# Side work of layer 1 tied on VectorE behind the two adds of each group

## The chip, the cores and the metric

The kernel runs on one core of a Trainium2 chip. The metric is the device time of one execution in microseconds (us); lower is better. PE is TensorE's matmul stream, PEld its weight loads, DVE is VectorE, ACT is ScalarE, POOL is GpSimd, SP is the engine whose queue issues all the DMAs.

## The reference

Three stages follow each other on 4608 tokens:

```python
# block-diagonal attention, chunks of 64, 8 heads of 64
attn = softmax(scale * q_c @ k_c.T); x = attn @ v_c         # [4608, 512]
# layer 1: 512 -> 2048 -> 512
r = maximum(x @ w_in, 0); x = (s * r * r + b) @ w_out
# layer 2: 512 -> 2048 -> 512, a rational function of h
h = x @ w2_in
g = (a0 + a1 h + a2 h^2 + a3 h^3) / (1 + |b0| |h| + |b1| h^2 + 1e-6)
out = g @ w2_out
```

Inputs are float32; the weights of layer 1 and 2 come in as 64-bit numbers, which DVE turns into float32 by shifts.

## The kernel before, in words

Every matrix product is made of float16 pairs (high and low part, three products each). The first product of a layer goes by a Strassen scheme: seven products p1 to p7 of half-size blocks, each 12 matmuls of 256 columns (L446), summed in two PSUM banks Z and Y. The second product (`l1_y2`, L485) has 48 matmuls of 512 columns per group.

Layer 1 runs over ten blocks j of tokens. Blocks 0 and 1 (256 tokens each) go in plain float32 while the weights are decoded. Blocks 2 to 9 (512 tokens) take four groups u = 0 to 3 each, `l1_group`; these 32 groups are called **G0 to G31** here (Gn is block 2 + n // 4, u = n % 4). PE's work in one group, in order: p1, p7, 15 matmuls L485 of the group before, p2, p6, 15 more, p4, p5, 12 more, p3, 6 more. Between them stand small matmuls of the attention of later blocks: the scores (L264) and the products with v (`at_pv`, L312).

Two adds on DVE close p4 and p5: L519 adds p7 to bank Y, **L520** adds it to bank Z. p3 writes bank Z, so PE may start p3 only after L520; the 12 matmuls L485 before p3 are what PE has to do meanwhile. On ACT each group has two evacuations after p1 and p7 (L505, L506), two after p2 and p6 (L513, L514; p4 needs L514), one after p3 (L527), and for each half of the group a Relu, a square and a cast (L522, L492, L493), whose result DVE reads (L494).

Everything else in layer 1 is side work: attention of later blocks (`at_*`: L275 and L276 subtract a maximum, L277 exp, L284 to L291 probabilities, L247 and L248 the split of v, L316 and L317 the result x), the split of x into pieces (`x_piece`, L402 to L416; pieces for p1, p7, p2, p5, p6, p4, p3 in this order), the output y of the block before (`y_norm`, `y_piece`, L567, L402 to L416), decoding and parking layer 2's weights (`w2_park`: L142, L144, L145, L586, then a DMA; one raw buffer of two units, loaded again by SP after every second unit), and constants of layer 2 (`l2_consts`, L658 to L677, 24 instructions on one or a few columns). These jobs are put in slots by hand, 16 slots per block, four per group; `jobs_at(n, c)` in `l1_group` issues slot n of the group, and its ACT instructions are queued behind the ACT instruction c.

The order on each engine is made at build time by a list scheduler with a cost model: the program's order gives the priority, but an instruction that looks ready early may be pulled ahead of others. `tc.issue_after(ins)` forbids that: what is issued in it on the engine of `ins` stands behind `ins` in that engine's queue. No time is spent by it on the chip; it is an order alone. The queues of DVE, ACT and PE then run in that order.

Of the kernel before, what the change touches and what calls it, by code (L numbers as in the profile page):

```python
# [13 lines left out]
ALU = mybir.AluOpType  # L14
# [6 lines left out]
def attn_moe_moe2(ctx: ExitStack, tc: tile.TileContext, qk, v, w_in, w_out, s_in, b_in,  # L21
# [57 lines left out]
    V, A, G, T = nc.vector, nc.scalar, nc.gpsimd, nc.tensor  # L79
# [358 lines left out]
    def product(w, x, u, p, b, start, stop=False):  # L438
        wk, pk = PROD[p]
        for s in range(2):  # L440
            f = 2 * u + s
            for kk in range(2):
                t = w.sh[wk, kk, f // 4]
                for n, (a, l) in enumerate(TERMS):
                    o = (f % 4) * 128
                    T.matmul(out=b[:, s, :], lhsT=t[:, a, o:o + 128], rhs=x[pk][:, l, kk, :],  # L446
                             start=start and s + kk + n == 0, stop=stop and s + kk + n == 4,
                             skip_group_check=True)
# [26 lines left out]
    crit = {}  # L475
# [14 lines left out]
    def l1_half(h, g):  # L490
        hf = h.rearrange("p s b t -> p (s b t)")
        A.activation(out=hf, in_=hf, func=AF.Square)  # L492
        A.activation(out=g[:, 0], in_=hf, func=AF.Copy)  # L493
        V.tensor_tensor(out=g[:, 1], in0=hf, in1=g[:, 0], op=ALU.subtract)  # L494

    def l1_group(j, u, jobs_at, m2):
        x = xhl[j]
        bank = lambda nm: ps_h.tile([128, 2, 256], F32, name=nm, tag="h")
        half = lambda: l1_p.tile([128, 2, 2, 256], F32, name="h1", tag="h1")
        jobs_at(0, crit.get("h"))  # L500
        Z, Y = bank("bZ"), bank("bY")
        product(wi1, x, u, "1", Z, True)
        product(wi1, x, u, "7", Y, True)
        p7 = l1_p.tile([128, 2, 256], F32, name="sn", tag="sn", bufs=3)
        A.activation(out=p7, in_=Y, func=AF.Copy)  # L505
        c = A.activation(out=Y, in_=Z, func=AF.Copy)  # L506
        m2(0)
        jobs_at(1, c)
        product(wi1, x, u, "2", Y, False)
        product(wi1, x, u, "6", Z, False)  # L510
        h0, h1 = half(), half()
        g = gq[j, u] = g_p.tile([128, 2, 2, 1024], F16, name="g", tag="g")
        A.activation(out=h0[:, :, 0], in_=Y, func=AF.Relu, scale=16.0 * C1)  # L513
        c = A.activation(out=Y, in_=Z, func=AF.Copy)  # L514
        m2(1)
        jobs_at(2, c)
        product(wi1, x, u, "4", Y, False, True)
        product(wi1, x, u, "5", Z, False)
        V.tensor_tensor(out=h1[:, :, 0], in0=Y, in1=p7, op=ALU.add)  # L519
        V.tensor_tensor(out=h1[:, :, 1], in0=Z, in1=p7, op=ALU.add)  # L520
        h1f = h1.rearrange("p s b t -> p (s b t)")
        A.activation(out=h1f, in_=h1f, func=AF.Relu, scale=16.0 * C1)  # L522
        l1_half(h1, g[:, :, 1])
        m2(2)
        jobs_at(3, c)
        product(wi1, x, u, "3", Z, False, True)
        crit["h"] = A.activation(out=h0[:, :, 1], in_=Z, func=AF.Relu, scale=16.0 * C1)  # L527
        l1_half(h0, g[:, :, 0])
        m2(3)
        if u == 3:  # L530
            xhl.pop(j)
# [62 lines left out]
    def w2_fetch(q):  # L594
        kk, g = q
        t = raw_p.tile([128, 4, 512], F32, name="wq", tag="raw")
        for i, u in enumerate(((kk, g), (kk + 2, g), (kk, g + 2), (kk + 2, g + 2))):
            nc.sync.dma_start(out=t[:, i, :], in_=wi2.dr[u])
        quad[q] = t
# [28 lines left out]
    def w2_combo(q, p):  # L628
        combo(wi2, [quad[q][:, i, :] for i in range(4)], q, p, (w2sc, w2nsc), w2_p if q[1] == 0 else wi1a_p, ws_raw)
# [101 lines left out]
    def run_jobs(slot):  # L731
        for fn, args in jobs.pop(slot, []):
            fn(*args)
# [21 lines left out]
    for j in range(NFULL, NB):  # L755
        at(start[j] + 3, l1_alpha, j)
        slot = start[j] + 1 - (PV0 if j > NFULL else P0)
# [48 lines left out]
    if True:  # L806
# [95 lines left out]
        def l1_slot(slot, after):  # L902
            j, k = slot // KF, slot % KF
            with tc.issue_after(after.ins) if after else ExitStack():
                run_jobs(slot)
            if j == NB - 1:
                if k >= 6:
                    wo2.fetch(wo2.todo.pop(0))
                if k >= 8:
                    wo2.split(wo2.cut.pop(0))  # L910
                for n in range(28 * k // KF, 28 * (k + 1) // KF):
                    q = quads[n // 7]
                    w2_combo(q, WORD[n % 7])
                    if n % 7 == 6 and n // 7 + 1 < 4:
                        w2_fetch(quads[n // 7 + 1])

        for j in range(NFULL, NB):
            if j == NB - 1:
                right.close()
                w2_p = ctx.enter_context(tc.tile_pool(name="w2", bufs=14, side="right", reuse_waits="tile"))  # L920
                w2_fetch(quads[0])
            for u in range(4):
                l1_group(j, u, lambda n, c: l1_slot(start[j] + 4 * u + n, c), m2_of(prev))
                prev = (j, u)
# [17 lines left out]
        def new_bank(i, k):  # L942
            pool, tag = {"Z": (ps_h, "h"), "Y": (ps_a, "s"), "C": (ps_a, "x")}[k]
            bank[i, k] = pool.tile([128, 2, 256], F32, name="b" + k, tag=tag)
            return bank[i, k]
# [76 lines left out]
        for i in range(N):  # L1022
            for q in range(4):
                step, slot = i + 2, q
                if i == 0:
                    step, slot = ((2, 2), (2, 3), (2, 3), (3, 0))[q]
                elif i == 1:
                    slot = q
# [21 lines left out]
        for i in range(N + 2):  # L1050
            cur, c = i < N, i - 1
            sl = (parts if c in (0, N - 1) else full) if 0 <= c < N else []
            if cur:
# [5 lines left out]
                Z, Y = new_bank(i, "Z"), new_bank(i, "Y")  # L1059
# [73 lines left out]
```

## Time and profile before

| what | value |
|---|---|
| time, median of 3 runs | 1589.96 us (1589.4 to 1591.37) |
| profiled execution, its own time | 1589.04 us |
| its span in the profile | 1587.2 us |
| PE busy over the span | 1538.0 us (97%) |
| DVE busy over the span | 1314.2 us (83%) |
| layer 1 in blocks 2 to 9 (G0 to G31) | about 160 to 870 us |
| layer 2 | about 870 to 1587 us |

How to read it: PE is busy nearly all the time, so time is saved where PE waits or runs at the lower clock. A row of the timeline gives the start, the duration, the engine, the line, what is written and read, how many instructions were merged into the row, and in brackets the idle time of the engine before it and what released it. A row of matmuls starts when the first is issued; the next row starts when PE issues the next one, so the difference of two starts is the time a piece of work takes in the stream.

### The profile page before, as it was taken

What the parts mean: (1) busy time and instruction counts of PE and PEld (TensorE: products, weight loads), DVE (VectorE), ACT (ScalarE), POOL (GpSimd) and SP (SyncE); (2) the same over time, 40 slices, a digit from 0 to 9 for tenths busy, and PEclk for the clock granted to TensorE, in tenths of its full rate; (3) what the DMA queues carried; (4) which work ended last, traced back from release to release, by engine and by line L of the source; (5) the groups of instructions that cost most, each with busy time, mean ns of one, the idle gap of its engine ahead of it and who ended that gap; (6) DMA issues with size and microseconds to landing.
All of it is one profiled execution on the core that took longest, in us unless ns stands there. A gap on an engine that the chain in (4) does not pass through costs nothing.

```text
span 1587.2 us, 29579 instructions
## 1 busy us (share of the span) xinstructions
PE 1538.0 (97%) x12497; PEld 1040.0 (66%) x12501; DVE 1314.2 (83%) x1980; ACT 963.2 (61%) x1268; POOL 25.4 (2%) x57
## 2 busy tenths in 40 slices
PE   7999999899899999999999899999999999999998
PEld 6878666566566666666666665666666666666664
DVE  7987989889877666665685999999888999999887
ACT  3565957556566666665675765555656565656564
POOL 0000000000000000000000000000000000000000
PEclk8999999999999999999999999999999999999999
DMA  7731345555532231312143020101010101011000
GB/s 283 274 87 55 93 138 160 197 167 172 174 101 87 61 95 29 106 28 54 47 133 114 13 75 34 47 27 47 27 47 28 47 27 47 31 44 35 26 27 27
DMA packets 86118, 131.43 MB, mean 83 GB/s; under 512 B 39648, under 2 KB 39648, under 8 KB 85984
## 3 DMA queue, kind: packets, MB, share of 16 engines
q1 hardware_dynamic: 85984, 129.53, 26.0%
q8 instruction: 98, 1.61, 0.4%
q14 instruction: 36, 0.29, 0.1%
HBM read 86.77 MB, written 34.34 MB: 76 GB/s over the span
## 4 chain that ended last, share of the span: by engine, by line
PE 59%; DVE 26%; DMA 5%; ACT 5%; issue 4%; SPq 0%; POOL 0%; DVEq 0%; ACTq 0%; POOLq 0%
PE y L1004 18%; PE bZ L446 15%; PE y L485 12%; PE bY L446 9%; PE bC L446 2%; DVE wf L145 2%; DVE bits L144 2%; DMA raw<-in_moe_w_in_dram 2%; DMA raw<-in_moe_w_out_dram 1%; DVE bits L142 1%; DVE whl L622 1%; DVE e L972 1%; DVE e L992 1%; DVE e L971 1%; DVE v L986 1%
## 5 line engine op out<-in xcount | busy, mean ns | idle before, releaser
L446 PEld LDWEIGHTS <-whl 128*128 128x128 f16 x5712 | 556.8, 98 | 145.4 <-issue 33.5
L446 PE MATMUL bZ<-xhl,whl 128*128 128x256 f16 x3264 | 405.8, 275 | 19.7 <-DVE h L520 14.8
L1004 PE MATMUL y<-whl,g 128*128 128x512 f16 x1728 | 396.2, 379 | 4.8 <-DVE g L993 3.5
L485 PE MATMUL y<-g,whl 128*128 128x512 f16 x1536 | 356.0, 382 | 0.1
L1004 PEld LDWEIGHTS <-g 128*128 128x128 f16 x1728 | 168.6, 98 | 180.7 <-DVE g L993 5.0
L485 PEld LDWEIGHTS <-whl 128*128 128x128 f16 x1536 | 151.3, 98 | 156.2 <-issue 3.4
L446 PE MATMUL bY<-xhl,whl 128*128 128x256 f16 x2016 | 248.5, 273 | 3.8 <-ACT h L527 1.7
L1093 ACT ACTIVATE h<-bZ 128x512 f32<-128x512 f32 x36 | 21.5, 597 | 226.5 <-PE bZ L446 172.6
L494 DVE TENSOR_TENSOR g<-h,g 128x1024 f16<-128x1024 f32 x64 | 78.2, 1222 | 54.8 <-ACT g L493 54.5
L970 DVE SCALAR_TENSOR_TENSOR v<-v,c 128x2048 f32<-128x2048 f32 (+1 forms) x42 | 85.8, 2044 | 33.0 <-ACT v L961 33.0
L522 ACT ACTIVATE h<-h 128x1024 f32<-128x1024 f32 x32 | 33.8, 1057 | 114.7 <-DVE h L520 114.7
L971 DVE TENSOR_TENSOR e<-e,h 128x2048 f32<-128x2048 f32 (+1 forms) x42 | 83.1, 1981 | 11.8 <-ACT e L962 11.7
L985 DVE SCALAR_TENSOR_TENSOR g<-e,na,r 128x2048 f16<-128x2048 f32 (+1 forms) x42 | 85.7, 2045 | 5.6 <-ACT r L977 2.5
L972 DVE SCALAR_TENSOR_TENSOR e<-e,na,h 128x2048 f32<-128x2048 f32 (+1 forms) x42 | 85.8, 2045 | 0.9
L992 DVE SCALAR_TENSOR_TENSOR e<-e,na,v 128x2048 f32<-128x2048 f32 (+1 forms) x42 | 85.6, 2042 | 0.7
L962 ACT ACTIVATE e<-h,na 128x2048 f32<-128x2048 f32 (+1 forms) x42 | 77.3, 1842 | 11.5 <-DVE g L993 11.4
L986 DVE SCALAR_TENSOR_TENSOR v<-v,g 128x2048 f32<-128x2048 f32 (+1 forms) x42 | 83.2, 1984 | 0.9
L961 ACT ACTIVATE v<-h,bc 128x2048 f32<-128x2048 f32 (+1 forms) x42 | 73.7, 1758 | 15.1 <-DVE h L1087 14.1
L993 DVE TENSOR_TENSOR g<-e,r 128x2048 f16<-128x2048 f32 (+1 forms) x42 | 82.8, 1976 | 0.0
L976 ACT ACTIVATE r<-v,c 128x2048 f32<-128x2048 f32 (+1 forms) x42 | 73.5, 1755 | 3.9 <-DVE v L970 3.9
L977 ACT ACTIVATE r<-r,c 128x2048 f32<-128x2048 f32 (+1 forms) x42 | 73.5, 1757 | 1.0
L493 ACT ACTIVATE g<-h 128x1024 f16<-128x1024 f32 x64 | 67.4, 1053 | 1.0
(189 smaller groups left out, 1808.1 us busy)
## 6 DMA issues: line engine op xcount, KB each, us to landing
qk<-in_qk_dram SPq DMA_DIRECT2D x36, 512.0 KB, 3.9
raw<-in_moe_w_in_dram SPq DMA_DIRECT2D x16, 1024.0 KB, 5.9
raw<-in_moe_w_out_dram SPq DMA_DIRECT2D x16, 1024.0 KB, 5.2
v<-in_v_dram SPq DMA_DIRECT2D x36, 256.0 KB, 2.7
out_dram<-o SPq DMA_DIRECT2D x36, 256.0 KB, 2.1
yd<-yhl SPq DMA_DIRECT2D x27, 256.0 KB, 2.1
xhl<-yd SPq DMA_DIRECT2D x27, 256.0 KB, 2.6
w2din<-wf SPq DMA_DIRECT2D x16, 256.0 KB, 2.1
```

What stands on the lines that cost most here:

```text
L446: T.matmul(out=b[:, s, :], lhsT=t[:, a, o:o + 128], rhs=x[pk][:, l, kk, :], start=start and s + kk + n == 0, stop=stop and s + kk + n == 4 ...
L485: T.matmul(out=ybank[j][dd], lhsT=wo1.hl[f][:, o:o + 128], rhs=g[:, l], start=(first and m == 0), stop=(last and m == 2))
L494: V.tensor_tensor(out=g[:, 1], in0=hf, in1=g[:, 0], op=ALU.subtract)
L962: A.activation(out=e, in_=hh, func=AF.Identity, scale=na[:, 3:4], bias=na[:, 2:3])
L970: V.scalar_tensor_tensor(out=v, in0=v, scalar=dlt, in1=v, op0=ALU.add, op1=ALU.mult)
L971: V.tensor_tensor(out=e, in0=e, in1=hh, op=ALU.mult)
L972: V.scalar_tensor_tensor(out=e, in0=e, scalar=na[:, 1:2], in1=hh, op0=ALU.add, op1=ALU.mult)
L985: V.scalar_tensor_tensor(out=g[:, 0], in0=e, scalar=na[:, 0:1], in1=r, op0=ALU.add, op1=ALU.mult)
L986: V.scalar_tensor_tensor(out=v, in0=v, scalar=q0c, in1=g[:, 0], op0=ALU.add, op1=ALU.mult)
L992: V.scalar_tensor_tensor(out=e, in0=e, scalar=na[:, 0:1], in1=v, op0=ALU.add, op1=ALU.subtract)
L993: V.tensor_tensor(out=g[:, 1], in0=e, in1=r, op=ALU.mult)
L1004: T.matmul(out=ybank[j][t], lhsT=g[:, a, q, t * 128:(t + 1) * 128], rhs=w[:, l * 512:(l + 1) * 512], start=(u + q == 0 and m == 0), stop=( ...
```

## The change

`jobs_at(2, c)`, the third slot's side work, is issued after the two adds and no longer ahead of p4. And the second add (now L519 in the changed file, L520 before) is kept as `crit["v"]`; all side work of a slot is put behind the latest such add on DVE. So slots 2 and 3 of a group stand behind this group's adds, slots 0 and 1 behind those of the group before. The weights' last steps in block 9 (`wo2.split`, `w2_combo`) stay outside.

```diff
         c = A.activation(out=Y, in_=Z, func=AF.Copy)
         m2(1)
-        jobs_at(2, c)
         product(wi1, x, u, "4", Y, False, True)
         product(wi1, x, u, "5", Z, False)
         V.tensor_tensor(out=h1[:, :, 0], in0=Y, in1=p7, op=ALU.add)
-        V.tensor_tensor(out=h1[:, :, 1], in0=Z, in1=p7, op=ALU.add)
+        crit["v"] = V.tensor_tensor(out=h1[:, :, 1], in0=Z, in1=p7, op=ALU.add)
+        jobs_at(2, c)
...
         def l1_slot(slot, after):
             j, k = slot // KF, slot % KF
             with tc.issue_after(after.ins) if after else ExitStack():
-                run_jobs(slot)
+                with tc.issue_after(crit["v"].ins) if "v" in crit else ExitStack():
+                    run_jobs(slot)
```

The changed file has one line less ahead of the adds, so lines 517 to 520 before are 516 to 519 after; L513 and L514 keep their numbers. The order of the instructions moves at these places.

DVE before, the end of G5: a decode of layer 2's weights (`bits`) stands between the two adds of h_3753.

```order
L288 TENSOR_TENSOR e<-e,rs 128x512
L416 SCALAR_TENSOR_TENSOR yhl<-tx,c_256,yhl 128x512
L108 TENSOR_SCALAR inv<-ape 128x1
L408 TENSOR_TENSOR tx<-y_3557 128x512
L109 RECIPROCAL sc<-inv 128x1
L519 TENSOR_TENSOR h_3753<-bY,sn 128x2x256
L142 TENSOR_SCALAR bits<-raw 128x512
L144 SCALAR_TENSOR_TENSOR bits<-raw,bits 128x512
L520 TENSOR_TENSOR h_3753<-bZ,sn 128x2x256
L145 SCALAR_TENSOR_TENSOR wf<-raw,bits 128x512
```

DVE after, the same two adds (L518 and L519 here) and what follows them.

```order
L109 RECIPROCAL c_256<-c_248 128x1
L570 TENSOR_SCALAR c_256<-c_256 128x1
L518 TENSOR_TENSOR h_3753<-bY,sn 128x2x256
L519 TENSOR_TENSOR h_3753<-bZ,sn 128x2x256
L275 TENSOR_REDUCE mx<-sp 128x4 x2
L276 TENSOR_TENSOR e<-sp,mx 128x4x64 x2
L416 SCALAR_TENSOR_TENSOR yhl<-y_3557,c_256,yhl 128x512
L402 TENSOR_TENSOR tx<-y_3557 128x512
L104 TENSOR_SCALAR apm<-amx 128x1
L142 TENSOR_SCALAR bits<-raw 128x512
```

The next group's decode, which was pulled ahead of the second add, now comes ten rows behind it; the adds stand together in nearly all groups.

DVE after, the end of G4 (h_3376): constants of layer 2 (c_269 and c_270 are two of their columns) stand between the side work and the adds. Before, these 24 instructions stood among the first decodes of the kernel, near 30 to 46 us.

```order
L288 TENSOR_TENSOR e<-e,rs 128x512
L675 TENSOR_SCALAR c_269<-c_269 128x1
L408 TENSOR_TENSOR tx<-y_1999 128x512
L673 RECIPROCAL c_270<-c_269 128x1
L291 TENSOR_TENSOR ph<-e,ph 128x512
L674 SCALAR_TENSOR_TENSOR c_269<-c_270,gb,c_269 128x1
L411 TENSOR_TENSOR y_1999<-tx,y_1999 128x2x256
L675 TENSOR_SCALAR c_269<-c_269 128x1
L416 SCALAR_TENSOR_TENSOR yhl<-tx,c_256,yhl 128x512
L673 RECIPROCAL c_270<-c_269 128x1
L518 TENSOR_TENSOR h_3376<-bY,sn 128x2x256
L674 SCALAR_TENSOR_TENSOR c_269<-c_270,gb,c_269 128x1
```

G4's stretch of DVE's queue, from the adds of G3 to those of G4, grows from 49 to 72 instructions.

ACT in G11 (u = 3, h_5556), around the evacuations L513 and L514, first before:

```order
L505 ACTIVATE sn<-bY 128x512
L506 ACTIVATE bY<-bZ 128x512
L290 ACTIVATE ph<-e 128x512
L415 ACTIVATE xhl<-x_4606,c_242 128x512
L415 ACTIVATE xhl<-tx,c_242 128x512
L513 ACTIVATE h_5556<-bY 128x2x256
L514 ACTIVATE bY<-bZ 128x512
L277 ACTIVATE e<-e 128x512
```

And ACT after, the same place:

```order
L505 ACTIVATE sn<-bY 128x512
L506 ACTIVATE bY<-bZ 128x512
L247 ACTIVATE vs<-v,sc 128x512
L415 ACTIVATE xhl<-x_4632,c_242 128x512
L415 ACTIVATE xhl<-tx,c_242 128x512
L290 ACTIVATE ph<-e 128x512
L513 ACTIVATE h_5556<-bY 128x2x256
L514 ACTIVATE bY<-bZ 128x512
```

L513 and L514 now stand behind L290, and on DVE L290's input (L288) and the scale c_242 (L392) have moved to the end of the group's queue, while before c_242 stood in its first half. All u = 3 groups from G7 to G23 have this order.

## Rows read from the trace of the kernel before

**Rows 1.** What PE waited for, 205 to 880 us (total, times, longest).

```profile
PE bZ L446 <- DVE h L520: 14.8, 6, 4.6
PE bY L446 <- ACT h L527: 1.7, 4, 0.9
PE bY L446 <- ACT bY L506: 1.1, 2, 0.6
```

**Rows 2.** Timeline of DVE at the end of G5.

```profile
286.73 0.43 DVE L142 TENSOR_SCALAR bits<-raw 128x512 int32<-128x512 int32 x1 [3.50 <-DMA raw<-in_moe_w_in_dram]
287.19 0.69 DVE L144 SCALAR_TENSOR_TENSOR bits<-raw,bits 128x512 int32<-128x512 int32 x1
287.80 0.68 DVE L520 TENSOR_TENSOR h<-bZ,sn 128x512 f32<-128x512 f32 x1
```

**Rows 3.** Timeline of PE: the 12 L485 of G1, p3 of G4, G5, G9.

```profile
187.48 2.75 PE L485 MATMUL y<-g,whl 128*128 128x512 f16 x12
261.66 1.47 PE L446 MATMUL bZ<-xhl,whl 128*128 128x256 f16 x12
288.53 2.72 PE L446 MATMUL bZ<-xhl,whl 128*128 128x256 f16 x12 [4.57 <-DVE h L520]
291.05 2.77 PE L485 MATMUL y<-g,whl 128*128 128x512 f16 x6
293.61 1.92 PE L446 MATMUL bZ<-xhl,whl 128*128 128x256 f16 x12
...
381.80 1.47 PE L446 MATMUL bZ<-xhl,whl 128*128 128x256 f16 x12 [1.35 <-DVE h L520]
```

**Rows 4.** Timeline of PE around p3 of G12.

```profile
450.55 2.75 PE L485 MATMUL y<-g,whl 128*128 128x512 f16 x12
453.14 1.47 PE L446 MATMUL bZ<-xhl,whl 128*128 128x256 f16 x12
454.45 1.46 PE L485 MATMUL y<-g,whl 128*128 128x512 f16 x6
```

**Rows 5.** Timeline of DVE: L520 of G16 and of G20.

```profile
535.72 0.69 DVE L520 TENSOR_TENSOR h<-bZ,sn 128x512 f32<-128x512 f32 x1
...
620.69 0.69 DVE L520 TENSOR_TENSOR h<-bZ,sn 128x512 f32<-128x512 f32 x1
```

**Rows 6.** Busy time by stretch: PE, PEld, DVE, ACT, POOL, PEclk, DMA share, GB/s.

```profile
290.00:300.00 10.00, 10.00 (x51) 5.62 (x49) 9.41 (x15) 8.21 (x12) 0.00 (x0) 0.77 0.59 209
300.00:400.00 100.00, 96.27 (x945) 64.14 (x945) 87.92 (x190) 58.16 (x89) 3.91 (x7) 0.98 0.57 178
500.00:600.00 100.00, 100.00 (x981) 66.76 (x979) 68.21 (x156) 63.67 (x98) 3.43 (x8) 1.00 0.27 75
```

**Rows 7.** Groups of DVE instructions, 205 to 870 us: busy, mean ns | idle before.

```profile
L494 DVE TENSOR_TENSOR g<-h,g 128x1024 f16<-128x1024 f32 x60 | 73.3, 1222 | 54.8 <-ACT g L493 54.5
L275 DVE TENSOR_REDUCE mx<-sp 128x4 f32<-128x256 f32 x46 | 17.3, 416 | 4.4 <-PE sp L264 4.4
L142 DVE TENSOR_SCALAR bits<-raw 128x512 int32<-128x512 int32 x30 | 12.6, 420 | 16.1 <-DMA raw<-in_moe_w_in_dram 8.4 <-DMA raw<-in_moe_w_out_dram 7.5
```

**Rows 8.** Timeline of DVE: decodes with constants between them, and without.

```profile
40.11 0.43 DVE L142 TENSOR_SCALAR bits<-raw 128x512 int32<-128x512 int32 x1
40.45 0.21 DVE L674 SCALAR_TENSOR_TENSOR c<-c,gb,c 128x1 f32<-128x1 f32 x1
40.58 0.68 DVE L144 SCALAR_TENSOR_TENSOR bits<-raw,bits 128x512 int32<-128x512 int32 x1
...
42.02 0.43 DVE L142 TENSOR_SCALAR bits<-raw 128x512 int32<-128x512 int32 x1
...
48.33 0.42 DVE L142 TENSOR_SCALAR bits<-raw 128x512 int32<-128x512 int32 x1
...
50.24 0.43 DVE L142 TENSOR_SCALAR bits<-raw 128x512 int32<-128x512 int32 x1
```

**Rows 9.** Timeline of PE: the column sums of w_out in G3.

```profile
228.83 3.35 PE L558 MATMUL cs<-one,whl 128*128 128x1 f16 x128
232.04 1.77 PE L446 MATMUL bY<-xhl,whl 128*128 128x256 f16 x12
```

**Rows 10.** Timeline of ACT and PE in G15 (u = 3).

```profile
504.49 0.72 ACT L415 ACTIVATE xhl<-x,c 128x512 f16<-128x512 f32 x1 [0.71 <-DVE c L392]
507.37 0.60 ACT L513 ACTIVATE h<-bY 128x512 f32<-128x512 f32 x1 [1.55 <-PE bY L446]
508.68 0.58 ACT L514 ACTIVATE bY<-bZ 128x512 f32<-128x512 f32 x1 [0.71 <-PE bZ L446]
511.66 1.47 PE L446 MATMUL bY<-xhl,whl 128*128 128x256 f16 x12
```

## The prediction

> **What bounds the kernel now.** I read the busy shares first: PE works over 97% of the span, so time can only come from PE's waits and from its clock. The table of PE's waits in layer 1 then says where these are [rows 1]: 14.8 us in six waits of p3 for L520, the second add on DVE; what waits for ACT is 2.8 us together. The timeline of DVE at the largest one [rows 2] shows why the add is late: a decode of layer 2's weights, L142, had stood ahead of it and waited 3.50 us for its DMA. DVE's queue runs in order, so the add waited too, and PE 4.57 us [rows 3]. What an idle stretch costs besides is seen in the two rows that follow on PE: 12 matmuls take 2.52 us from 288.53 to 291.05 where they take 1.31 in G12 [rows 4], and the clock of 290 to 300 us is 0.77 of 2.4 GHz [rows 6], so part of it at the lower level, 1.2 GHz. Against undisturbed work (1.31, 1.30, 1.31) the three pieces to 295.36 (the next start) lose 1.2 + 1.3 + 0.4 = 2.9 us. After 1.35 us of idle at 381.80 the matmuls have their normal 1.47 [rows 3]: nothing is lost.
>
> Where these waits lie: from p3 of G4 (261.66) to p3 of G12 (453.14) [rows 3, 4] the kernel takes 191.5 us for two blocks. A block without waits takes 620.69 - 535.72 = 84.97 [rows 5], two take 169.9. So 21.5 us are lost in these two blocks, and nearly nothing in the four after them. The stretches say why there [rows 6]: DVE is 88% busy at 300 to 400 us and 68% at 500 to 600, since the scheduler pulls all decodes as far ahead as the raw buffer lets it.
>
> **What the change does to DVE's queue.** It removes nothing. I count DVE's queue between two L520 in the new order, with these prices: an instruction of 1024 columns takes 1.22 us and starts the next 0.07 earlier, so 1.15; 512 columns 0.69, so 0.61 to 0.67 (start to start 0.61 from 287.19 to 287.80 [rows 2]); 256 columns 0.34 [rows 7]; a one-column one 0.08 to 0.13 with a large one behind it [rows 8]. In blocks 4 to 7 the four groups come to 14.3, 17.9, 14.7 and 18.8 us, against some 21.2 us of PE's time. The decodes are spread, one or two per group, and each stands some 8 us or more behind the one that frees the raw buffer. So the DMA that took 16.1 us of DVE's time in all [rows 7] is mostly in time, and where it isn't, 2.4 us or more of slack in DVE's queue and the 2.6 us of the 12 L485 [rows 4] stand before PE feels it. All six waits of [rows 1] should go. If one decode still waits 3.5 us, as in [rows 2], the price is 0 to 1 us.
>
> **What is late next.** I went through each group of one block with these prices and the two queues ACT and DVE side by side. For u = 0, 1, 2 PE's next need (L506 before p2, L514 before p4, the add before p3) is met with 0.7 us or more to spare. For u = 3 it isn't. In G11 DVE's queue up to L288 is 2 x 1.15 + 16 x 0.63 + 6 x 0.34 + 15 x 0.08 = 15.6 us; it starts 0.8 us after the 12 L485 and waits some 0.6 for ACT and POOL: 17.0. ACT's L415, L415, L290 follow, and L513 and L514 behind them end at 19.2. PE wants p4 at 18.6 by its own work. It waits 0.6 us. Bounds: nothing if DVE runs without a wait, 3.5 if a decode waits for its DMA as in [rows 2]; I take 0.6, since DVE's raw buffer there was loaded about 15 us earlier. Five groups (G7, G11, G15, G19, G23): 3.0 us.
>
> The price of ACT's strict order is in [rows 10]: L415 waited 0.71 us for c, and L513 stood behind it, yet L514 started 3.0 us before p4 (508.68 and 511.66). The Trainium skill, "PSUM — Partial Sum Buffer", section "Engine vs sequencer instructions", calls the queues of ScalarE and VectorE strict FIFO, which speaks against this change: what VectorE's new order delays, ScalarE's evacuations wait out. The trace agrees as far as that row goes; by the rule alone the cost is 0 or the whole wait of L290, 0.6 here.
>
> **The start of layer 1.** In G0 the attention's work leaves the way of the adds: by hand about 2 us less. In G1 ACT gets the second product with v and two splits ahead of L506, some 1.7 us more. Together 0.3 gained, bounds -3 and +3.
>
> G2 and G3 lose their small waits. But the queue of G4 holds 72 instructions: 2 x 1.15 + 33 x 0.63 + 6 x 0.34 + 31 x 0.08 = 27.8 us, more than a group of PE. It starts 0.8 us after the 12 L485 of G3 and waits about 1.5 for the column sums (PE, 3.2 us [rows 9]) and 0.5 elsewhere: L519 stands at 30.5, p3 at 31.25. Up to those 12 L485, from those of G1, PE has 96 L485 (0.216 each by [rows 4], 20.7), 14 products (1.31 each, 18.3) and 3.0 of attention: 42.0. Sum 73.3 where the trace has 261.66 - 187.48 = 74.2 [rows 3]: 0.9 gained.
>
> Of the tiny constants [rows 8] show that they cost nothing where they stood: a decode takes 42.02 - 40.11 = 1.91 us with three of them in it and 50.24 - 48.33 = 1.91 without, so nothing comes back there; in G4 they cost some 2 us, contained above. The Trainium skill, "Advanced Engine Details and Errata", "The Read-Write Bubble", has the memory latency exposed between instructions on VectorE, each paying it; by that rule 24 instructions at their 0.15 would give back 3.6 us at the start, and the sum would end 3.6 lower. The row says otherwise for this chain.
>
> In G5 the two products with v that were delayed come close together, and the second waits for ACT's copy of the first (0.8), and p2 for L506 (1.1): 1.9 us. Bounds 0 and 4.6, the longest wait of [rows 1]. One clock dip behind the 2 us of waiting in G4: between 0 (381.80) and 2.9 (288.53), I take 1.6.
>
> **Sum.** Two blocks after: 169.9 + 0.9 (one product with v that now lies behind p3 of G4) + 1.9 + 2 x 0.6 = 173.9, so 17.6 gained. With 0.9 and 0.3, less 3 x 0.6 for the later blocks and 1.6 for the clock: 15.4 us. The profiled execution took 1589.04, so 1573.6; the median of the runs is 0.9 above it: 1574.5, and I say 1575. Layer 2's queues have the same order, and block 9's splits stand as before; I take nothing there, bounds -2 and +2.
>
> **Rivals.**
> - No new wait at all. All excess goes: 21.5 + 2 for G0 to G3: 1567. For it: DVE's slack in [rows 6]; against it: G4's 27.8 us.
> - The first two blocks cost double. Hand sums leave out waits between ACT and DVE; twice the 1.9, 1.6 and 31.25 - 29 of G4: about 6 more, 1581.
> - The waits change place and stay: decodes that wait for DMA fill DVE's slack in every group, so nearly the whole 21.5 comes back elsewhere: 1588. Against it, DMA has 16.1 us of waits in all [rows 7].
> - Slower: L514 behind L290 in the u = 3 groups. If DVE's chain to L288 there ends 3 us later than I count (a decode at 3.5 us of wait in each), PE waits 3.6 us and loses about 0.9 by its clock in each of five groups: 5 x 3.9 = 19.5 on top, 1594. It decides from about 3.1 us more per group on. For it: four engines' waits meet in that chain, two decodes among them; against it: both units come with one DMA that is started a group before.
>
> **How the numbers follow.** My forecast (1571 to 1579) gets 0.48, no new wait 0.14, double cost 0.21, waits that stay 0.06, slower 0.11. About 0.2% (3.2 us) is what a measurement of this kernel can tell from no change. So faster 0.83, within it 0.06, slower 0.11. The range 1565 to 1588 leaves out the slower case and the far ends.
>
> **What would show it.** Right: p3's waits for L520 gone or under 1 us between 265 and 450 us, two L520 four groups apart by about 85.5 us in blocks 3 to 7, DVE's busy share near 75% there and even, one wait of about 2 us in G4 and 1 to 2 in G5, and in every u = 3 group a wait of p4 for L514 of about half a microsecond. Wrong: L142's waits for DMA as large as before and PE still waiting for the second add; waits of p4 for L514 of 2 us and more; or a new wait of p2 for L506 in all u = 1 groups.

## The result and the profile after

The changed kernel takes 1571.58 us (median of four runs, 1570.5 to 1573.38). The kernel before took 1589.68 beside it, and the ratio is 0.9893 [0.9878, 0.9909] (in brackets, here and below, the 95% interval): faster by 1.1%. The forecast was 1575, in a range of 1565 to 1588. The profiled execution took 1570.5 us with a span of 1568.7, against 1589.04 and 1587.2: 18.5 us less in both.

The table of PE's waits comes first, 205 to 880 us of the changed kernel (total, times, longest); it answers [rows 1].

```profile
PE bY L446 <- ACT h L527: 2.2, 3, 1.3
PE bZ L446 <- DVE h L519: 1.9, 3, 0.9
PE y L485 <- ACT y L548: 1.2, 1, 1.2
```

The wait for the second add (L519 here) fell from 14.8 us to 1.9. A new one of 1.2 us, for ACT's copy L548, lies in G5.

DVE at the end of G5, against [rows 2]:

```profile
279.16 0.69 DVE L518 TENSOR_TENSOR h<-bY,sn 128x512 f32<-128x512 f32 x1
280.18 0.69 DVE L519 TENSOR_TENSOR h<-bZ,sn 128x512 f32<-128x512 f32 x1 [0.33 <-PE bZ L446]
...
283.44 0.42 DVE L142 TENSOR_SCALAR bits<-raw 128x512 int32<-128x512 int32 x1
```

DVE now waits for PE and no longer PE for DVE. The decode starts 3.26 us behind the add, and no wait stands ahead of it: its DMA has landed. Over all of layer 1 the groups of DVE instructions (205 to 870 us, as in [rows 7]) say the same:

```profile
L494 DVE TENSOR_TENSOR g<-h,g 128x1024 f16<-128x1024 f32 x60 | 73.2, 1221 | 8.0 <-ACT g L493 7.2
L142 DVE TENSOR_SCALAR bits<-raw 128x512 int32<-128x512 int32 x32 | 13.4, 420 | 1.3 <-DMA raw<-in_moe_w_in_dram 1.3
```

The idle time ahead of L142, nearly all of it for its DMA, went from 16.1 to 1.3 us. That ahead of L494, where DVE waits for ACT's cast, went from 54.8 to 8.0: the last decode starts at 650.51 us and no longer at 435.42, so decodes fill that time. The busy time by stretch (PE, PEld, DVE, ACT, POOL, granted clock, DMA share, GB/s), against [rows 6]:

```profile
290.00:300.00 10.00, 10.00 (x95) 6.41 (x93) 4.35 (x9) 3.70 (x7) 0.35 (x1) 1.00 0.88 263
300.00:400.00 100.00, 100.00 (x1019) 66.48 (x1018) 80.08 (x180) 64.51 (x96) 3.28 (x7) 1.00 0.39 120
500.00:600.00 100.00, 100.00 (x974) 66.10 (x973) 75.50 (x165) 60.98 (x94) 2.89 (x7) 1.00 0.40 122
```

DVE's load is even (80% and 76%, from 88% and 68%), PE has no idle time in these stretches, and the clock of 290 to 300 us is full where it was 0.77.

PE at the places of [rows 3, 4]: the 12 L485 of G1, p3 of G4, G5, and p3 of G12.

```profile
185.84 2.75 PE L485 MATMUL y<-g,whl 128*128 128x512 f16 x12
...
254.43 4.05 PE L485 MATMUL y<-g,whl 128*128 128x512 f16 x18
258.32 0.82 PE L446 MATMUL bZ<-xhl,whl 128*128 128x256 f16 x6
259.62 2.12 PE L446 MATMUL bZ<-xhl,whl 128*128 128x256 f16 x18 [0.48 <-DVE h L519]
...
267.49 3.46 PE L485 MATMUL y<-g,whl 128*128 128x512 f16 x15 [1.23 <-ACT y L548]
...
431.51 1.47 PE L446 MATMUL bZ<-xhl,whl 128*128 128x256 f16 x12
```

The six matmuls at 258.32 are not p3: they are the first half of p1 of G5, which PE's new order puts ahead of p3 and which needs the bank that the first add frees. In a second execution (below) the same six start at 260.36, before the second add does (261.07). p3 of G4 is the first 12 of the 18 at 259.62. From there to p3 of G12 it is 431.51 - 259.62 = 171.9 us, from 191.5. But 1.95 us of PE's work (six L485 and half of p1) now lie ahead of p3 of G4 that stood behind it before; like for like it is 173.8, where 173.9 had been worked out.

Not all is gain. In block 7 the changed kernel loses what the forecast did not have. DVE ahead of the adds of G23:

```profile
663.97 0.69 DVE L608 TENSOR_TENSOR ws<-wq 128x512 f32<-128x512 f32 x1 [3.69 <-DMA wq<-w2din]
664.70 0.69 DVE L609 TENSOR_TENSOR wq<-wq 128x512 f32<-128x512 f32 x1
665.31 0.69 DVE L518 TENSOR_TENSOR h<-bY,sn 128x512 f32<-128x512 f32 x1
665.91 0.68 DVE L519 TENSOR_TENSOR h<-bZ,sn 128x512 f32<-128x512 f32 x1
```

L608 is the first combination of block 9. It isn't among the tied jobs, so it stands where decodes stood before: ahead of the adds, waiting for its DMA. In the kernel before, it had come as early as G12, when the decodes were done:

```profile
445.61 0.69 DVE L608 TENSOR_TENSOR ws<-wq 128x512 f32<-128x512 f32 x1 [2.18 <-DMA wq<-w2din]
```

The adds of G12 followed at 450.27, and PE didn't wait for them. With the decodes spread, the same instruction comes 218 us later. Between L519 of G20 and of G24 there are 87.63 us here, against 84.97 between the L520 before.

### The profile page after: what moved, and what is told of

Its sections match the earlier page's. It is cut to its first block, busy times and chain, and to the rows that moved or that the text cites. A ratio compares the mean times of both kernels' runs of the same rounds, so it can differ in the third digit from the quotient of the medians.

```text
span 1568.7 us, 29641 instructions
## 1 busy us (share of the span) xinstructions
PE 1533.7 (98%) x12501; PEld 1037.9 (66%) x12501; DVE 1307.2 (83%) x1980; ACT 960.0 (61%) x1268; POOL 22.9 (1%) x57
## 4 chain that ended last, share of the span: by engine, by line
PE 74%; DVE 16%; ACT 5%; issue 3%; DMA 1%; POOL 0%; SPq 0%; DVEq 0%; ACTq 0%; POOLq 0%
PE y L1005 19%; PE bZ L446 18%; PE y L485 17%; PE bY L446 11%; PE bC L446 2%; PE y L468 1%; PE hp L455 1%; PE xp L312 1%; DVE whl L622 1%; DVE e L973 1%; DVE e L993 1%; PE sp L264 1%; DVE v L987 1%; DVE g L994 1%; DVE g L986 1%
## 5 line engine op out<-in xcount | busy, mean ns | idle before, releaser
L446 PEld LDWEIGHTS <-whl 128*128 128x128 f16 x5712 | 555.1, 98 | 130.8 <-issue 19.1
L446 PE MATMUL bZ<-xhl,whl 128*128 128x256 f16 x3264 | 402.2, 273 | 5.4 <-DVE h L1086 2.1
L485 PE MATMUL y<-g,whl 128*128 128x512 f16 x1536 | 355.0, 380 | 1.2 <-ACT y L548 1.2
L485 PEld LDWEIGHTS <-whl 128*128 128x128 f16 x1536 | 150.4, 98 | 155.4 <-issue 2.6
L446 PE MATMUL bY<-xhl,whl 128*128 128x256 f16 x2016 | 248.3, 273 | 3.9 <-ACT h L527 2.6
L518 DVE TENSOR_TENSOR h<-bY,sn 128x512 f32<-128x512 f32 x32 | 22.1, 690 | 102.8 <-PE bY L446 102.8
L494 DVE TENSOR_TENSOR g<-h,g 128x1024 f16<-128x1024 f32 x64 | 78.1, 1221 | 8.2 <-ACT g L493 7.4
L962 ACT ACTIVATE v<-h,bc 128x2048 f32<-128x2048 f32 (+1 forms) x42 | 73.7, 1758 | 14.8 <-DVE h L1088 13.8
```

What stands on the lines that cost most here:

```text
L485: T.matmul(out=ybank[j][dd], lhsT=wo1.hl[f][:, o:o + 128], rhs=g[:, l], start=(first and m == 0), stop=(last and m == 2))
```

## The experiments

Three theories were put up. A: the loss was a decode that waits for its DMA ahead of the second add. B: it was the third slot's work, queued ahead of p4 and the adds. C: it was the amount of side work ahead of the adds, and any spreading helps. B and C are rivals of the prediction's reading. A fourth, F, concerns ACT's order in the u = 3 groups. Where a kernel ran with others its kernel before had a median of 1588.9 to 1591.4, so ratios are compared.

**The two edits apart.** The tie alone:

```diff
+        crit["v"] = V.tensor_tensor(out=h1[:, :, 1], ...)   # jobs_at(2, c) stays ahead of p4
...
+                with tc.issue_after(crit["v"].ins) if "v" in crit else ExitStack():
+                    run_jobs(slot)
```

> Only the tie: side work stands behind the two adds of the group before, but the third slot's work is still issued ahead of p4 and of the group's own adds. Theory A (the loss was decodes that wait for their DMA ahead of the second add): the decodes stand as in the changed kernel, one or two per group, so 1570 to 1575 us, p3's waits for the second add under 2 us in all between 265 and 640 us. Theory B (the loss was the third slot's work that was queued ahead of the adds): nothing gained, 1586 to 1590. Theory C (any work that is spread evenly over the groups helps, and both edits spread it): between, about 1578 to 1582.

Measured: 1569.29 us, ratio 0.9864 [0.9848, 0.9880]. The whole gain; that it is more can't be told, since the intervals touch.

The move alone:

```diff
-        jobs_at(2, c)
...
         V.tensor_tensor(out=h1[:, :, 1], in0=Z, in1=p7, op=ALU.add)
+        jobs_at(2, c)
```

> Only the move: the third slot's work comes behind the adds in the program, and nothing is tied. Theory A: the decodes are still pulled ahead, three to four per group in G2 to G11, so the waits of p3 for the second add stay (12 to 17 us) and the time is 1585 to 1591 us. Theory B: nearly the whole gain, 1571 to 1575. Theory C: 1578 to 1582.

Measured: 1595.77 us, ratio 1.0036 [1.0024, 1.0049]: slower, and 5 us above what A expected. B falls, and so does C where it says that any spreading helps. PE's waits of this kernel, 205 to 880 us:

```profile
PE bZ L446 <- DVE h L519: 18.8, 6, 4.7
```

**The tie taken apart.** Only the decodes tied (the third slot not moved), and everything but the decodes (moved):

```diff
         for fn, args in jobs.pop(slot, []):
-            fn(*args)
+            with tc.issue_after(crit["v"].ins) if "v" in crit and fn is w2_park else ExitStack():
+                fn(*args)          # the other kernel: fn is not w2_park
```

> Of all side work only the decodes of layer 2's weights (with their loads and stores) are tied behind the adds; the third slot stays ahead of p4; the constants of layer 2 stay at the start of the kernel. Theory A: the whole gain, 1568 to 1574 us: G4's queue is 48 instructions and not 72, so the wait for the copy L548 in G5 (1.2) and for the add in G4 (0.5) go, and the first adds of G23 still wait for L608. Theory B: 1586 to 1590. Theory C (the attention's and the splits' work matters as much as the decodes): half the gain, 1578 to 1582.

Measured: 1567.91 us, ratio 0.9855 [0.9838, 0.9871]. More than the whole gain, from the decodes alone (its interval lies below that of the changed kernel).

> The changed kernel with the decodes set free: all other side work is tied and the third slot's work is moved, but the decodes may run ahead and two to four instructions of one stand between the two adds of most groups from G4 to G18. Theory A: most of the loss is back, spread over more groups, since each hoisted decode waits for its DMA ahead of the second add: 1583 to 1592 us, DVE's wait of L142 for DMA again 10 us or more. Theory B: the gain stays, 1571 to 1575. Theory C: half, 1577 to 1582.

Measured: 1615.71 us, ratio 1.0155 [1.0130, 1.0181]: 25 us slower than before, a price that no theory had. The group of the decodes' first instruction, and PE's waits, 205 to 870 and 205 to 880 us:

```profile
L142 DVE TENSOR_SCALAR bits<-raw 128x512 int32<-128x512 int32 x30 | 12.5, 417 | 55.3 <-DMA raw<-in_moe_w_out_dram 28.7 <-DMA raw<-in_moe_w_in_dram 26.6
```

```profile
PE xp L312 <- DVE e L276: 12.7, 8, 3.2
PE bZ L446 <- DVE h L519: 9.5, 9, 3.2
PE xp L312 <- DVE apm L104: 7.5, 3, 3.0
```

DVE waits 55.3 us for DMA, with nothing else to do, since the rest of the work may not pass the adds and the adds stand behind the decode. The end of G13 shows it:

```profile
478.85 0.43 DVE L142 TENSOR_SCALAR bits<-raw 128x512 int32<-128x512 int32 x1 [7.44 <-DMA raw<-in_moe_w_out_dram]
479.19 0.68 DVE L518 TENSOR_TENSOR h<-bY,sn 128x512 f32<-128x512 f32 x1
...
481.12 0.68 DVE L519 TENSOR_TENSOR h<-bZ,sn 128x512 f32<-128x512 f32 x1
```

The attention's first step (L276) is tied behind L519 and comes late too, and PE waits at L312 as well. So a tie on the rest without the decodes is worse than no tie.

**Wait or amount.** All but the first of the 16 loads of raw weights leave out 15/16 of the bytes, in the kernel before and in the kernel that ties everything but the decodes:

```diff
+            old = park_raw.get(0) if hasattr(self, "dr") else None
+            t = old or pool.tile([128, 2, 1024], I32, name="raw", tag=tag)
+            n = 64 if old else 1024
...
+            nc.sync.dma_start(out=t[:, :, 0:n], in_=src[:, :, 0:n])
```

> The kernel before, but of the 16 loads of layer 2's raw weights all but the first bring 64 of 1024 columns into one tile that stays (the decoded weights are wrong from the second load on; all instructions of DVE, ACT and PE are there). The scheduler now pulls the decodes ahead still more: about four per group from G5 to G10 and none from G11 on. Theory A (the cost is the decode's wait for its DMA ahead of the second add): with 1/16 of the bytes DVE's waits of L142 for DMA fall from 15.9 to under 6 us, p3's waits for L520 from 14.8 to under 6, and the time to 1574 to 1581 us. Theory C (the cost is the amount of DVE work pulled ahead of the adds, whatever the DMA does): 18 to 19 us of DVE work by my prices in each of G5 to G10, more than before, so L520's waits stay at 12 us or more and the time at 1586 to 1594.

Measured: 1582.66 us, ratio 0.9947 [0.9932, 0.9961], between the two. DVE's group and PE's wait (the lines lie 7 lower in this kernel: L149 is L142, L453 is L446 and L527 is the second add), and the stretch of 300 to 400 us:

```profile
L149 DVE TENSOR_SCALAR bits<-raw 128x512 int32<-128x512 int32 x30 | 12.6, 419 | 3.0 <-DMA raw<-in_moe_w_in_dram 2.6 <-DMA raw<-in_moe_w_out_dram 0.5
```

```profile
PE bZ L453 <- DVE h L527: 12.3, 10, 2.8
```

```profile
300.00:400.00 100.00, 92.87 (x895) 61.07 (x893) 95.15 (x207) 56.76 (x87) 5.75 (x8) 1.00 0.44 133
```

The DMA waits are nearly gone, and PE still waits 12.3 us for the second add, in ten waits instead of six. DVE is 95% busy: the decodes that no longer wait are pulled ahead more densely. So A alone is wrong: what costs is that decodes run ahead, with a wait or without. The kernel before says it too, read again. Its PE waited here, and between the adds of G6 and G7 DVE has no wait for DMA but 0.66 us at 310.67:

```profile
335.25 2.54 PE L446 MATMUL bZ<-xhl,whl 128*128 128x256 f16 x12 [2.13 <-DVE h L520]
```

By the ratios 8.4 of about 23 us (decodes tied: 0.9855) came back, in an order that was denser than before. But PE's waits for the add fell by 2.5 us only, from 14.8 to 12.3. Most of the rest goes with the granted clock. In the kernel before it falls behind three of the six waits, in G5, G7 and G11 (290 to 300 us: 0.77; 330 to 340: 0.83; 430 to 440: 0.83), where the matmuls take 2.9, 1.7 and 1.7 us longer, 6.3 in all. With the short loads it is 1.00 from 240 to 470 us, behind a wait of 2.82 us too:

```profile
334.41 1.47 PE L453 MATMUL bZ<-xhl,whl 128*128 128x256 f16 x12 [2.82 <-DVE h L527]
```

So the DMA's own waits gave back little of PE's waiting. That they gave back the clock isn't shown: the length of a wait doesn't tell whether it falls (last section). The order changed with the loads, so a clean share of wait and amount can't be read off.

> The same short loads in the kernel that ties everything but the decodes (it took 1615.7 us, with 55 us of waits of L142 for DMA). The decodes are pulled ahead to three per group and pieces of them stand between the two adds up to G12. Theory A: without the long loads these waits fall under 10 us and the time to 1575 to 1584, though the order is as bad as in the kernel with whole loads. Theory C: the order alone costs, 1595 us or more.

Measured: 1597.45 us, ratio 1.0045 [1.0030, 1.0060]. 18 of the 25 us come from the loads, yet DVE still waits 24.8 us for the short loads and 16.6 us in L145 for the stores of decoded weights. The time lies where C had it (1595 or more), but A's condition, waits under 10 us, did not come about, so this run does not tell A from C.

**ACT's order in the u = 3 groups.** Three more reductions ahead of L284 there, and ACT's order held:

```diff
+        if tile_block[t][0] > NFULL and tile_block[t][1] == 0:
+            for _ in range(3):
+                V.tensor_reduce(out=sm, in_=e, axis=AX.X, op=ALU.add)
...
-        A.activation(out=ph[:, 0], in_=e, func=AF.Copy)
+        crit["ph"] = A.activation(out=ph[:, 0], in_=e, func=AF.Copy)
...
+        with tc.issue_after(crit["ph"].ins) if u == 3 and 1 < j < NB - 2 else ExitStack():
+            A.activation(out=h0[:, :, 0], in_=Y, func=AF.Relu, scale=16.0 * C1)
```

> The changed kernel with three more reductions (the same sum again, about 0.6 us each) on DVE ahead of L284 in the groups with u = 3 from G3 to G23, and ACT held to the changed kernel's order there (L290 ahead of L513 and L514). Theory F (ACT's order is strict, and in the changed kernel L514 comes 0.1 us late, as the trace has it: end 405.0, PE's own time for p4 404.95): p4 waits 1.6 to 2.0 us for L514 in each of G7, G11, G15 and G19, and up to that in G3 and G23, so 7 to 11 us more than the changed kernel if the clock holds (1578 to 1583), and up to 2.9 us more for each wait if it falls. Rival (there is slack of a microsecond that this trace does not show): waits under 1 us, 1571 to 1575.

Measured: 1585.29 us, ratio 0.9979 [0.9963, 0.9994]: 1.8 us more DVE work in each of six groups takes 14 of the 17 us back. PE's wait, 205 to 880 us, and ACT and PE in G15 (3 to 4 lines lower: L293 is L290, L517 and L518 are L513 and L514, L449 is L446):

```profile
PE bY L449 <- ACT bY L518: 10.8, 5, 2.2
```

```profile
498.13 0.63 ACT L293 ACTIVATE ph<-e 128x512 f16<-128x512 f32 x1 [2.94 <-DVE e L291]
498.66 0.58 ACT L517 ACTIVATE h<-bY 128x512 f32<-128x512 f32 x1
499.27 0.58 ACT L518 ACTIVATE bY<-bZ 128x512 f32<-128x512 f32 x1
```

```profile
499.91 2.26 PE L449 MATMUL bY<-xhl,whl 128*128 128x256 f16 x12 [2.15 <-ACT bY L518]
501.97 2.39 PE L449 MATMUL bZ<-xhl,whl 128*128 128x256 f16 x12
```

L517 had its input since PE's 493.49 (p2 and p6 were done) and stood behind L293 until DVE was done. F holds; the waits lie in G7, G11, G15, G19 and G23, each 2.15 to 2.16 us, a little above the range, and behind two of them the clock fell. The edit did more than add 1.8 us: on DVE the scheduler put the two splits L419 (L416 in the changed kernel) among the reductions, ahead of L291, so that L518 starts 5.78 us behind the end of p6 (493.49) where its like started 2.73 behind it in the changed kernel's G15, 3.05 earlier. On PE it put 19 matmuls of the second product between p6 and p4 and no longer 15, 0.86 us more. The difference is 2.2 us, which is the wait. In the changed kernel the same place has no wait to speak of:

```profile
402.69 0.71 ACT L415 ACTIVATE xhl<-tx,c 128x512 f16<-128x512 f32 x1
403.31 0.61 ACT L290 ACTIVATE ph<-e 128x512 f16<-128x512 f32 x1
403.83 0.57 ACT L513 ACTIVATE h<-bY 128x512 f32<-128x512 f32 x1
404.43 0.58 ACT L514 ACTIVATE bY<-bZ 128x512 f32<-128x512 f32 x1
```

L514 ends at 405.01 and p4 starts at 405.06. PE's own work would have let it start at 401.70 + 3.24 = 404.94 (the start of the 15 L485 behind p6, and what they take from start to start where nothing waits). The margin is used up to 0.1 us.

**Mending what is left.** The constants handed out at the start again, and block 9's combinations tied too:

```diff
-    at(start[3], l2_consts)
+    at(0, l2_consts)
...
+                    with tc.issue_after(crit["v"].ins):
-                    w2_combo(q, WORD[n % 7])
+                        w2_combo(q, WORD[n % 7])
```

> The changed kernel with two more edits: the constants of layer 2 are handed out at the start again, and block 9's combinations of layer 2's weights (the first waited 3.69 us for its DMA ahead of the adds of G23) are tied behind the adds like the other side work. Theory A: G23 gives back 2.6 us (period 24.12 to 21.4 to 21.9), G4 and G5 the waits of 0.5 and 1.2 to 1.5: 1566 to 1569 us, a ratio of about 0.986 to 0.9875. Rival: the wait for L608 only moves into G24, and the constants cost at the start what they give back later: 1570 to 1573, ratio 0.9885 to 0.990.

Measured: 1567.41 us, ratio 0.9854 [0.9837, 0.9871]. DVE at G23 and PE at G4:

```profile
661.48 0.69 DVE L518 TENSOR_TENSOR h<-bY,sn 128x512 f32<-128x512 f32 x1 [1.64 <-PE bY L446]
662.72 0.69 DVE L519 TENSOR_TENSOR h<-bZ,sn 128x512 f32<-128x512 f32 x1 [0.55 <-PE bZ L446]
```

```profile
257.76 2.64 PE L446 MATMUL bZ<-xhl,whl 128*128 128x256 f16 x12 [2.10 <-DVE h L519]
```

G23's period (add to add) falls from 24.12 to 21.36, and G24's grows by 0.23: 2.5 us back, as expected. From G3 to G6 only 0.6 come back, and p3 of G4 waits longer than in the changed kernel. What had hidden it there is the 1.95 us of other work ahead of p3, and a clock dip (a stretch at the lower clock) on PE behind the column sums (230 to 240 us: 0.83), which made PE 1.7 us late too (235.09 to 239.37, against 236.64 to 239.24 for the same work without the dip). A second profiled execution of the changed kernel (span 1571.8, below) has no dip there (1.00), and PE waits first for the bank that the first add frees and then, at p3, for the second:

```profile
260.36 0.81 PE L446 MATMUL bZ<-xhl,whl 128*128 128x256 f16 x6 [2.00 <-DVE h L518]
261.81 3.79 PE L446 MATMUL bZ<-xhl,whl 128*128 128x256 f16 x18 [0.64 <-DVE h L519]
```

```profile
261.07 0.68 DVE L519 TENSOR_TENSOR h<-bZ,sn 128x512 f32<-128x512 f32 x1
```

The 18 matmuls that took 2.12 us in the first execution take 3.79 here. So DVE's chain bounds G4, and what PE shows of it depends on its clock. From L560 (behind the column sums) to the second add the chain takes 23.84 and 24.47 us with the constants (the two executions of the changed kernel), 21.83 and 21.79 without (two of this one). That is the price of the constants, 2.0 to 2.7 us, DVE's waits in the chain included. In the second pair, without a dip behind the sums in either, G3 to G6 takes 73.26 and 70.53 us: 2.7 back.

The last four kernels ran on one chip. The new one ties only decodes and combinations, and moves the third slot's work in G0 alone:

```diff
+        if not ((j, u) == (NFULL, 0)):
+            jobs_at(2, c)
...
+        if (j, u) == (NFULL, 0):
+            jobs_at(2, c)          # behind the two adds
```

> Only the decodes and block 9's combinations are tied behind the adds, and the third slot's work is moved behind them in G0 alone, where the move let the second add of G0 and G1 come 4.0 and 1.3 us earlier. Theory A with the pieces added up: against the kernel that ties the decodes alone 1.3 us for G1, 0.3 to 1.3 for the waits of p3 in G23 and G30: 1565 to 1567.5 us. Rival: G0's order costs in G1 to G3 what it gains (as with the move alone, where G1 to G3 took 2 us more), and it is the decode kernel again, 1567 to 1570.

> The changed kernel again, on the chip of the three others: 1570 to 1574 us.

> The kernel that ties the decodes alone, again: by the profiles' spans (1567.3 and 1568.7) 1.4 us under the changed kernel, by the ratios to the kernel before 6 us; between them, 2 to 5 us under it. If it is the same within 1 us, the ties of the other side work neither help nor cost.

> The changed kernel with the constants at the start and the combinations tied, again: 3.3 us under the changed kernel by the spans (1565.4 and 1568.7), 6 by the ratios: 3 to 5 under it here.

Measured, with 1588.9 for the kernel before: 1564.95 (0.9841 [0.9820, 0.9863]); the changed kernel 1573.54 (0.9891 [0.9870, 0.9911]); decodes alone 1566.53 (0.9852 [0.9830, 0.9873]); constants and combinations 1566.2 (0.9852 [0.9830, 0.9873]). The first beats both kernels of this case, by 24 and 8.6 us. Against the decodes alone its 1.6 us are at the low end of what was expected, and the intervals overlap. The changed kernel is 7 us above the kernel that ties the decodes alone, which "2 to 5" had too small. In the profiled executions it loses 5.4 us between the adds of G0 and G20 and 4.7 between those of G20 and G31, is 2.0 ahead at G0 and 1.5 faster behind G31. With the constants and the combinations mended the loss is gone (1566.2 and 1566.53), though the move and the ties of all other work are still there. So the 7 us are, in the main, the price of those two places. The tie without the move is 1.4 us above the decodes alone (1569.29 and 1567.91), within the noise. What the kernel of 1564.95 us has left of PE's waits in layer 1 (160 to 900 us) for the adds is

```profile
PE bZ L446 <- DVE h L521: 1.7, 3, 0.7
```

## Why the prediction was right, and where its terms were off

It was right in place and in the mechanism of an add behind decodes that run ahead; the sum of 15.4 us stands against 18.5 of the profiled executions. Term by term, from the starts of the same work, for both profiled executions of the changed kernel against the one of the kernel before (the second ran on another chip):

| term | worked out | first | second | from (before, first, second) |
|---|---|---|---|---|
| G0 and G1 | +0.3 | +1.64 | +0.11 | 12 L485 of G1: 187.48, 185.84, 187.37 |
| from there to p3 of G4 | +0.9 | +0.40 | -0.26 | 74.18, 73.78, 74.44 |
| p3 of G4 to p3 of G12 | +17.6 | +19.59 | +18.89 | 191.48, 171.89, 172.59 |
| clock behind G4 | -1.6 | 0 | -1.7, in the row above | 260 to 270 us: 1.00 and 0.83 |
| p3 of G12 to the last second add | -1.8 | -3.68 | -4.29 | 395.43, 399.11, 399.72 |
| from there to the end | 0 | +0.5 | +0.9 | 738.6, 738.1, 737.7 |

Of the third row 1.95 us belong to the second (the work that now lies ahead of p3 of G4): like for like the two are +2.35 and +17.64 in the first execution. The second adds up to 15.4, the forecast to the tenth, and that is luck: its terms are off by up to 2.5 us and cancel. (The 27.8 us of G4's queue add up to 27.6 by the prices given.)

- **The bound.** The waits of p3 for the second add were the ones to go, and they went: the six of 14.8 us are three of 1.9. The reading of [rows 2], that the add is late because a decode ahead of it waits for DMA, was true of that wait and too narrow for all six: the short loads took most DMA waits away and left 12.3 us of PE's 14.8. What the forecast rested on was the other half of that paragraph, DVE's 88% in [rows 6]: decodes run ahead. Tying them alone gave everything.
- **DVE's even queue.** About 85.5 us per block were forecast, and 85.09 came in blocks 4 to 6, 84.2 in block 3 and 87.6 in block 7; DVE's share is 80 and 76% where 75% was named.
- **The wait in G4.** About 2 us at p3 and 1.6 for the clock behind it were forecast. The first execution shows 0.48 and no dip there, because the clock had already fallen behind the column sums (1.7 us) and because PE's new order has six more L485 (18 in a row at 254.43) and half of p1 ahead of p3, which the forecast did not count. The second shows 2.64, of which 0.64 at p3, and the dip (260 to 270 us: 0.83, 1.7 us). The DVE queue had been priced to within 1 us: behind the 12 L485 of G3 the second add was put at 30.5 and came at 29.6 and 30.2. Which of PE's losses comes first varies from run to run.
- **G5.** 1.9 us were forecast from two waits, for the copy of the products with v and for L506. Measured are 0.28 for the copy of the first product (L316, forecast 0.8), nothing for L506 (1.1), and 1.23 for another copy, L548, which the forecast did not have: the size nearly right, the cause mostly wrong.
- **u = 3.** The term was 0.6 us in five groups; it is 0.1. The place is right, and the 3 us of slack that L514 had in [rows 10] are gone. On the forecast's clock (from the start of G10's 12 L485, 386.32) L288 ended at 16.75 where 17.0 was worked out, L514 at 18.69 for 19.2, and p4's own time was 18.62 for 18.6. Half a microsecond of prices, half of it on DVE and half on ACT, was the whole term. That the mechanism is real the run with three reductions shows: 2.15 us of wait in each of five groups, and 14 us in all, for L514 about 3 us later. The rival that ended slower had its mechanism right, and it lacked the delay; with it, it would have been too dear (19.5 us), partly since PE's four more matmuls fill 0.86 us of each wait.
- **ACT's queue.** The Trainium skill, "PSUM — Partial Sum Buffer", section "Engine vs sequencer instructions", calls these queues strict FIFO. The trace agrees: L517 stood behind L293, which waited 2.94 us.
- **The tiny constants.** [rows 8] said that the 24 instructions cost nothing at the start. In the kernel that hands them out there again a decode takes 1.92 us with three of them in it and 1.90 without (40.33 to 42.25 and 48.55 to 50.45), and its two executions have L519 of G0 at 165.49 and 167.67, against 165.37 and 166.89 in the changed kernel: 0.1 and 0.8 us, within what two executions of one kernel differ. The Trainium skill, "Advanced Engine Details and Errata", "The Read-Write Bubble", would have had 3.6 us for them by the estimate of the forecast; in this chain no run shows it.
- **Layer 1's end.** "Block 9's splits stand as before" was the step that failed: L608 moved from 445.61, in G12, to 663.97, ahead of the adds of G23, and waits 3.69 us for its DMA. The -1.8 of that row was meant for u = 3, which took 0.1 per group; what stands in it instead is this. From G20's add to G24's this takes 2.66 us, and 1.76 more are lost from there to the last add of G31. (0.36 from G12 to G20 come to it; the table's 3.68 begins at p3 of G12 and is 1.1 less than a count from the adds, since a product with v now lies between the two.) The run that tied the combinations gave 2.5 and 0.7 back.

## What to carry to other kernels

When a scheduler fills an in-order queue, look for work that it may run ahead as far as a buffer allows, and tie that work behind the operation for which the bounding engine waits; a tie on the rest adds nothing here, and costs where it pushes other work into a full queue or lets an untied wait stand ahead (the constants and L608, 7 us together with the move); one that leaves out the work with the DMA waits is worse than none. Work out what stands behind each wait on both queues, the waiting engine's own order included: an evacuation behind an operation that waits for another engine has only the slack that was there before. A wait for DMA in a queue may be the visible part alone; load by stretch shows the rest.

## What the runs showed of the hardware that was not expected

What a wait of PE costs by the clock is not told by its length. In the kernel with three reductions p4 waits for L518 in five groups, 2.15 to 2.16 us in each, at the same place of a block. Behind the wait in G15 (above) the two products take 2.26 and 2.39 us; behind that in G11 they have their normal 1.47:

```profile
412.19 1.47 PE L449 MATMUL bY<-xhl,whl 128*128 128x256 f16 x12 [2.16 <-ACT bY L518]
413.50 1.47 PE L449 MATMUL bZ<-xhl,whl 128*128 128x256 f16 x12
```

```profile
410.00:420.00 10.00, 7.84 (x59) 5.67 (x58) 6.59 (x13) 7.17 (x12) 0.35 (x1) 1.00 0.18 40
...
500.00:510.00 10.00, 10.00 (x63) 6.84 (x63) 6.14 (x12) 5.94 (x10) 0.35 (x1) 0.83 0.15 28
```

By the add-to-add periods G11 takes 3.07 us more than in the changed kernel and G15 4.72. G7 is like the one and G19 like the other; behind G23's wait p4 takes 1.47 too. One kernel does both at one place: with the constants and the combinations mended, p3 of G4 took 2.64 us behind a wait of 2.10 in the first execution (above), and in the second

```profile
259.89 1.47 PE L446 MATMUL bZ<-xhl,whl 128*128 128x256 f16 x12 [2.07 <-DVE h L519]
```

In the kernel before, p3 takes 2.54 us behind 2.13 of waiting in G7 (above) and 1.47 behind 2.21 in G10. The column sums too leave the full clock behind them in one execution of the changed kernel (1.00) and not in the other (0.83). What decides it stays open.
